# Two token tiles transposed and multiplied at a time in 64-row tiles, in an infini-attention block, with a new order of all engines

## The chip, the cores and the metric

The kernel runs on one core of a Trainium2 chip. The metric is the device time of one execution in microseconds. Five engines have their own instruction streams: TensorE (PE in the profile: matrix products and transposes, with its weight loads as PEld), VectorE (DVE), ScalarE (ACT), GpSimd (POOL) and SyncE (SP, which only issues DMA transfers here). They wait for each other through semaphores. SBUF is the on-chip memory, PSUM the eight banks that TensorE writes its results to.

## The reference

One block on a sequence of 2048 tokens of width 512: layer norm with a scale and a shift from a condition vector c, an attention of 32 heads of 16 in four segments of 512 tokens with a compressive memory, a residual; then a second such norm, a feed-forward layer of width 1792 with a squared ReLU, and a residual.

```python
x = A_x                                             # [1, 2048, 512]
mod = (_silu(c) @ w_mod).reshape(c.shape[0], 6, 1, -1)
sa, ca, ga, sb, cb, gb = (mod[:, i] for i in range(6))
h = _layernorm(x) * (1 + ca) + sa
x = x + ga * _A_ref(h, A_wq, A_wk, A_wv, A_wo, A_beta)
h = _layernorm(x) * (1 + cb) + sb
x = x + gb * _B_ref(h, B_w1, B_b1, B_w2, B_b2)

# _A_ref: q, k, v = x @ wq, x @ wk, x @ wv, cut into heads of 16 and N = 4 segments
for s in range(N):
    p = _softmax(qs @ ks.T * scale + mask)          # causal within the segment
    a_mem = (phi(qs) @ M) / (phi(qs) @ z + 1e-6)    # phi(t) = t + 1 if t > 0 else exp(t)
    o = g * a_mem + (1 - g) * (p @ vs)              # g = sigmoid(beta)
    M, z = M + phi(ks).T @ vs, z + phi(ks).sum(0)
# o of all heads, [2048, 512], times wo

# _B_ref: relu(x @ w1 + b1) ** 2 @ w2 + b2
```

## The kernel before

**Numbers.** Products are made of float32 values split into a high half, a copy rounded to a format that TensorE takes (`fp32r`), and a low half, the value less the high one. A product is three: high by high, high by low, low by high. The high copy is made by ACT, the low by DVE or POOL, so every operand of a product has a pair "hi, lo" behind it (L618 for the normed tokens, L699 for weights, L1251 and L1253 for the heads' output).

**Shapes on TensorE.** A product or a transpose works in one of three modes. F uses all 128 rows. R uses tiles of 64 rows, two side by side, which take two products at a time. C (the products of probabilities and values, L1122) uses tiles of 32 columns. The rows `128*128`, `64*128` and `128*32` of the profile show them. A transpose is a product with an identity matrix; in F a token tile (128 tokens by 512) takes four of 128x128, in R a tile of 64 rows makes one of 64x64.

**Stages.** The sequence is 16 token tiles of 128, four to a segment s = 0 to 3.
- Head: x is loaded, the modulation made (`mod_parts`, `mod_cols`: `modc` holds scale and shift by column, L586), the first segment normed and transposed (`ln1(0)`, then `ln_transposed`), the weights wq, wk, wv split (`split_w`, its lows at L699 on POOL and DVE), and the first q and k made: in F for the first unit (L779 to L781, after the last `HT`), in R afterwards (L787).
- Attention: 16 units u, four heads-groups to a segment: `qk`, `vproj`, the maxima of the scores (`a_quad`), the exponentials and the products with the values (`b_quad`), the memory (`mem`). Each unit ends in transposes of its results (L1157, `bfin`) and DVE's norm and add (L1171 to L1180). The next segment's `ln1` runs in between.
- Output product: `wo_tile` (L1226) for each token tile. Its four F transposes into a bank `bwot` (L1245), the high copy on ACT (L1251), the low on DVE (L1253), twelve F products with wo into a bank `bwop` (L1218 to L1220), the residual x1 and its statistics on DVE (L1260, L592, L593). Tiles of segments 0 to 2 load their heads' output from DRAM; those of segment 3 take it from the tile `X1L`.
- Second norm: `ln2` (L1268), four F transposes a tile (L605) and the affines half on ACT (L1281), half on DVE (L1283), into `h2raw`.
- FFN: products in a scheme like Strassen's with seven instead of eight (`ffn1`, L1475; `ffn2`, L1539 to L1541), a residual on DVE (L1550), and the stores of the output by SP (L1552). The output of segments 0 to 2 stands in tiles `X`, that of segment 3 in `X1L`.

**What sets the order.** All work is held as nodes in one `Plan` (L239): an engine, an estimated duration, the nodes it comes after, the buffers that it takes and gives back, and for TensorE the mode. A table `ORDER` (L56) lists the node numbers of PE, ACT, DVE, POOL and SP in the sequence in which that engine runs them. Buffers come from pools that are counted: `#A` 8, `#B` 8, `#V` 2 and `#D` 5 bank uses within the 8 banks, `xr` 4 token tiles, `oT` 2 split tiles of the heads' output. The transposes and products of `ln_transposed` (other than the first segment), `wo_tile` and `ln2` take banks of `#D`. A fence (L760) is a one-element copy on ACT that TensorE waits for when it goes from writing one set of row tiles to another in the same banks.

## Time and profile before

| what | us |
|---|---|
| median of three runs | 796.09 |
| lowest, highest | 795.66, 796.46 |
| profiled execution, its own time | 795.43 |
| its span (first to last instruction) | 793.7 |
| PE busy | 764.5 |
| DVE busy | 599.3 |
| ACT busy | 441.7 |
| POOL busy | 323.4 |

The busy shares of 40 equal slices of the span show the stages; the columns are tenths, PEclk the granted clock of TensorE in tenths. The FFN is the part from slice 25 on.

```profile
PE   9899999989999999999999999999999999999995
PEld 8777666765677656787576669898989889889984
DVE  5688758978789678989988789787866876476543
ACT  2568967789878898686865653556121321121110
POOL 4576674688777887545342252442002010000000
PEclk9999989999999999999999999999999999999998
DMA  9576856542644533435452275665543454544613
```

The costliest groups of instructions, busy time and mean ns, then the idle time before them with what ended it:

```profile
L899 DVE CUSTOM_DVE_ANT_0 ba<-ba,msk 128x512 f32<-128x512 f32 (+2 forms) x384 | 192.3, 533 | 36.9 <-PE ba L894 23.3
L1080 ACT ACTIVATE pt<-bpb 128x512 f32<-128x512 f32 x320 | 173.7, 619 | 22.4 <-PE bpb L1063 19.1
...
L1475 PE MATMUL bh<-H2o,w 128*128 128x256 f32 x1176 | 157.8, 282 | 1.4 <-DVE h2raw L1283 0.8
```

A row reads: line, engine, operation, tile written and tiles read (tile names without buffer numbers; `b...` is a PSUM bank), shape and type, how often it ran.

### The profile page before, as it was taken

Reading aid. Unit: us, or ns where it says so; the run is one execution under the profiler, and the core shown is the slowest. Engines: PE = TensorE matmul, PEld = TensorE weight load, DVE = VectorE, ACT = ScalarE, POOL = GpSimd, SP = SyncE. Lnnn points to the kernel's source line nnn. Section 1 sums busy time; section 2 is a strip of 40 time slices with the busy share of each in tenths; the row PEclk is TensorE's granted clock in tenths of the full one; section 3 lists DMA queues with packets and bytes.
Section 4 is the critical chain, followed back from the end, with each engine's and each line's share of the span. In section 5 each row is a group of like instructions: output and inputs, shape, how many; then the busy total and the mean of one; then the engine's idle time right before and its main releaser. Section 6 shows DMA issues by size and latency. Waiting matters only on the chain.

```text
span 793.7 us, 18015 instructions
## 1 busy us (share of the span) xinstructions
PE 764.5 (96%) x6649; PEld 606.7 (76%) x6649; DVE 599.3 (76%) x1591; ACT 441.7 (56%) x1001; POOL 323.4 (41%) x400
## 2 busy tenths in 40 slices
PE   9899999989999999999999999999999999999995
PEld 8777666765677656787576669898989889889984
DVE  5688758978789678989988789787866876476543
ACT  2568967789878898686865653556121321121110
POOL 4576674688777887545342252442002010000000
PEclk9999989999999999999999999999999999999998
DMA  9576856542644533435452275665543454544613
GB/s 313 138 195 171 246 181 196 160 135 94 192 128 133 169 94 96 131 86 159 130 141 81 82 252 199 213 239 199 186 169 116 180 204 181 186 165 160 233 53 145
DMA packets 59265, 129.65 MB, mean 163 GB/s; under 512 B 8613, under 2 KB 23977, under 8 KB 55594
## 3 DMA queue, kind: packets, MB, share of 16 engines
q1 hardware_dynamic: 59026, 128.37, 50.3%
q8 instruction: 53, 0.87, 0.5%
q14 instruction: 34, 0.28, 0.1%
q10 hardware_dynamic: 152, 0.13, 0.1%
HBM read 81.29 MB, written 20.19 MB: 128 GB/s over the span
## 4 chain that ended last, share of the span: by engine, by line
PE 61%; ACT 8%; DVE 4%; DMA 2%; SPq 1%; issue 1%; POOL 1%; ACTq 0%; DVEq 0%; POOLq 0%
PE bh L1475 16%; PE bpf L1540 6%; PE bpf L1539 6%; PE bpf L1541 6%; PE bpv L1122 5%; PE bqk L787 4%; PE bpb L1063 3%; PE ba L894 3%; ACT pt L1080 3%; PE bv L860 2%; PE bwop L1218 2%; PE bwop L1220 2%; PE bwop L1219 2%; ACT lnf L611 1%; SPq L839 1%
## 5 line engine op out<-in xcount | busy, mean ns | idle before, releaser
L899 DVE CUSTOM_DVE_ANT_0 ba<-ba,msk 128x512 f32<-128x512 f32 (+2 forms) x384 | 192.3, 533 | 36.9 <-PE ba L894 23.3
L1080 ACT ACTIVATE pt<-bpb 128x512 f32<-128x512 f32 x320 | 173.7, 619 | 22.4 <-PE bpb L1063 19.1
L1475 PEld LDWEIGHTS bh<-H2o,w 128*128 128x128 f32 x1176 | 153.9, 189 | 11.6 <-ACT h2raw L1281 1.4
L1475 PE MATMUL bh<-H2o,w 128*128 128x256 f32 x1176 | 157.8, 282 | 1.4 <-DVE h2raw L1283 0.8
L1067 POOL TENSOR_SCALAR_AFFINE_SELECT pt<-pt 128x512 f32<-128x512 f32 x128 | 79.6, 638 | 87.7 <-ACT pt L1080 65.0
L787 PE MATMUL bqk<-HT,WQK 64*128 64x512 f32 x720 | 104.4, 399 | 0.0
L1521 ACT CAST rr<-xx 128x512 fp32r<-128x512 f32 x56 | 34.4, 620 | 97.3 <-DVE xx L1511 60.2
L894 PE MATMUL ba<-ST 63*128 63x256 f32 (+2 forms) x512 | 79.7, 351 | 5.5 <-DMA ST<-sg 1.4
L1122 PE MATMUL bpv<-pt,VT 128*32 128x512 f32 (+3 forms) x1024 | 83.7, 448 | 0.7 <-POOL pt L1067 0.4
L1063 PE MATMUL bpb<-ST 64*128 64x256 f32 (+2 forms) x512 | 80.4, 352 | 2.2 <-ACT e L828 0.7
L787 PEld LDWEIGHTS bqk<-HT,WQK 64*128 64x128 f32 x720 | 73.3, 187 | 6.5
L894 PEld LDWEIGHTS ba<-ST 63*128 63x128 f32 x512 | 51.4, 186 | 31.2 <-ACT pt L1080 7.1
L1063 PEld LDWEIGHTS bpb<-ST 64*128 64x128 f32 x512 | 52.5, 188 | 21.1 <-ACT pt L1080 4.7
L1539 PE MATMUL bpf<-w,rr 128*128 128x512 f32 x160 | 63.5, 397 | 0.0
L1540 PE MATMUL bpf<-w,rr 128*128 128x512 f32 x160 | 63.0, 393 | 0.0
L1541 PE MATMUL bpf<-w,rr 128*128 128x512 f32 x160 | 62.5, 391 | 0.0
L860 PE MATMUL bv<-WVO,HT 64*128 64x512 f32 x384 | 54.9, 397 | 0.0
L899 DVE DVE_READ_ACCUMULATOR2_ANT mx<- 128x1 f32 x384 | 54.3, 141 | 0.0
L1122 PEld LDWEIGHTS bpv<-pt,VT 128*32 128x32 f32 x1024 | 27.3, 110 | 33.7 <-issue 25.5
L1523 DVE TENSOR_TENSOR rr<-xx,rr 128x512 fp32r<-128x512 f32 x56 | 40.0, 720 | 12.7 <-ACT rr L1521 12.6
L1501 ACT COPY p<-bh 128x256 f32<-128x256 f32 x28 | 10.4, 371 | 63.2 <-PE bh L1475 34.9
L1498 DVE SCALAR_TENSOR_TENSOR u<-bh,b1c,u 128x256 f32<-128x256 f32 x56 | 26.9, 480 | 24.3 <-PE bh L1475 23.2
(171 smaller groups left out, 1459.8 us busy)
## 6 DMA issues: line engine op xcount, KB each, us to landing
w<-w1d SPq DMA_DIRECT2D x28, 1792.0 KB
ST<-sg SPq DMA_DIRECT2D x192, 128.0 KB
w1d<-X1L SPq DMA_DIRECT2D x21, 512.0 KB
xt<-in_A_x SPq DMA_DIRECT2D x16, 256.0 KB
wm<-in_w_mod SPq DMA_DIRECT2D x16, 256.0 KB
xw<-in_A_x SPq DMA_DIRECT2D x16, 256.0 KB
X1L<-in_B_w SPq DMA_DIRECT2D x7, 512.0 KB
wr<-in_B_w SPq DMA_DIRECT2D x14, 256.0 KB
```

What stands on the lines that cost most here:

```text
L787: nc.tensor.matmul(bank(banks[w]), W3(w, k, x, cols.start, cols.stop)[r], HT[r, y, k], start=turn == k == i == 0, stop=turn == 1 and k == ...
L860: nc.tensor.matmul(bank(banks[t]), HT[r, x, k, (t2 + t) * P:(t2 + t + 1) * P], WVO[r, k, y], start=turn == k == i == 0, stop=turn == 1 and ...
L894: nc.tensor.matmul(dst[:, c0:c0 + n], ST[b:b + 63, 0, sl, qt * P:(qt + 1) * P], ST[b:b + 63, 1, sl, :n], start=True, stop=True)
L899: nc.vector.tensor_tensor_reduce(i, i, msk[:, 512 - n:], scale=1.0, scalar=-3e38, op0=ALU.add, op1=ALU.max, accum_out=o)
L1063: nc.tensor.matmul(dst, ST[b:b + 64, 1, sl, kb * P:(kb + 1) * P], ST[b:b + 64, 0, sl, q0:512], start=True, stop=True)
L1067: nc.gpsimd.affine_select(out=ap, in_=ap, pattern=[[0, ap.shape[1]], [1, P]], compare_op=ALU.is_ge, fill=0.0, base=0, channel_multiplier=-1)
L1080: ns = [op("ACT", 0.49, lambda j=j: nc.scalar.activation(buf("PPP"[n], pt)[:, i + j], bank(keys[j]), AF.Exp, scale=0.25), pr[slot] + 0.01 ...
L1122: nc.tensor.matmul(bank(o)[32 * hq:32 * hq + 32, q0:q0 + src.shape[1]], v[:, a:a + 32], src, start=start, stop=stop, tile_position=(0, 32 ...
L1475: nc.tensor.matmul(pb(i), A[:, x, kk], B[:, y, kk], start=kk == j == 0, stop=kk == 1 and j == 2)
L1539: nc.tensor.matmul(q, rh, wh, start=(i == 0), stop=False)
L1540: nc.tensor.matmul(q, rh, wl, start=False, stop=False)
L1541: nc.tensor.matmul(q, rl, wh, start=False, stop=(i == NF - 1))
```

## The change

Three groups of token tiles are now handled two at a time, in R.

1. `ln_pair` takes the place of two `ln_transposed` for segments 1 to 3. The transposes of two tiles are one turn of 16, of 64 rows by 128, into two banks: the upper 64 rows of both tiles go to one, the lower to the other. ACT makes the affine of a whole bank, copies the high half into HT in strides, and POOL makes the low half.
2. `wo_pair` takes the place of two `wo_tile` for segments 0 to 2: two loads of heads, two of x; 16 R transposes into two banks; high and low copies per bank; 48 R products of 64 rows by 512 in two turns, with a fence between the turns. In the first turn the rows of tile half j go to bank j, in the second to the other. The pool `oT` has one tile, of twice the size. Tiles of segment 3 keep `wo_tile`.
3. `first_pair` transposes the second norm of segment 0 in two pairs.

In `ln_transposed` the low half is locked in the plan (`lock=True`), and the table `ORDER` is new for all engines.

In instructions: transposes of the first norm of 128x128 (bank `blnq`, from `xt`) 64 to 16, of 64 rows 0 to 96; of the second norm 64 to 48 and 0 to 32; of the output product (bank `bwot`, from `ot`) 48 to 0 and 0 to 96; products with wo of 128 rows 192 to 48, of 64 rows 0 to 288; one-element copies of the fence on ACT 8 to 14. All other counts stay. Along PE's order the shape changes 181 times before and 136 times now.

```diff
 ORDER = {
     "PE": """
-8-27 3 28-40 86 94 111 41 88 42-45 96 46-51 123 52 105 53 117 54-77 280-281 290 282-284 291-292 285 293 286 294 287
+8-20 3 21-38 105 111 94 86 39 96 88 40-52 117 53-56 123 57-70 290 71-73 291-292 74-77 293 280-282 294 283-287 295-297
...
-             "phi1": 2, "pk": 1, "am": 3, "on": 1, "mx": 2, "mt": 1, "oT": 2, "mv": 2, "ac": 1, "#F": 4, "xx": 3, "rr": 4, "wr": 3,
+             "phi1": 2, "pk": 1, "am": 3, "on": 1, "mx": 2, "mt": 1, "oT": 1, "mv": 2, "ac": 1, "#F": 4, "xx": 3, "rr": 4, "wr": 3,
...
-        l = op(low, 1.24 if low == "POOL" else 0.6, lambda: ln_split(dst(), t, TL[f], low)[1](), pr + 0.03, after=[h], put=[f])
+        l = op(low, 1.24 if low == "POOL" else 0.6, lambda: ln_split(dst(), t, TL[f], low)[1](), pr + 0.03, after=[h], put=[f], lock=True)
...
+    def ln_pair(s, g, src, sc, bi, pr, after, put, wait):
+        b, f = ([(n, sc, s, g, j) for j in (0, 1)] for n in ("lnq", "lnf"))
+        def turn():
+            for k in range(KD):
+                for i in (0, 1):
+                    for j in (0, 1):
+                        r, c_ = slice(64 * j, 64 * j + 64), k * P + 64 * i
+                        nc.tensor.transpose(bank(b[j])[:, c_:c_ + 64], src(i)[r, k * P:(k + 1) * P], ident[r, r])
+        n = pe("R", 0.522, turn, pr, after=after, get=[("#D", q) for q in b], put=put)
+        ends = []
+        for j in (0, 1):
+            a = op("ACT", 1.38, lambda j=j: ln_affine("av", buf("oraw", f[j]), bank(b[j]), sc, bi), pr + 0.01 + 0.01 * j,
+                   after=[n, *MODC[sc], *(wait if j else [])], get=[("oraw", f[j])], put=[b[j]])
...
+            h = act(512, lambda part=part, whole=whole: nc.scalar.copy(part(0), whole()), pr + 0.02 + 0.01 * j, sbuf=True,
+                    after=[a, *wait], put=[f[j]])
+            l = op("POOL", 1.24, lambda part=part, whole=whole: nc.gpsimd.tensor_tensor(part(1), whole(), part(0).bitcast(F32), op=ALU.subtract),
+                   pr + 0.03 + 0.01 * j, after=[h], put=[f[j]])
+            ends += [h, l]
+        return ends, a
...
+    def wo_pair(g, pr):
...
+        n = pe("R", 0.522, turn, pr, after=ld, get=[("#D", q) for q in b], put=o)
...
+        for j in (0, 1):
+            h = act(512, lambda j=j: nc.scalar.copy(part(0, j), whole(j)), pr + 0.01 + 0.005 * j, after=[n] + hl[:1],
+                    get=() if j else [("oT", ot)], put=[b[j]])
+            hl += [h, dve(512, lambda j=j: nc.vector.tensor_tensor(part(1, j), whole(j), part(0, j).bitcast(F32), op=ALU.subtract),
+                          pr + 0.012 + 0.005 * j, after=[h], put=[b[j]])]
+        def mm(turn, k):
+            for i, (x, y) in enumerate(((0, 0), (0, 1), (1, 0))):
+                for j in (1, 0) if turn else (0, 1):
+                    t, r = j ^ turn, slice(64 * j, 64 * j + 64)
+                    nc.tensor.matmul(bank(bo[t]), TL[ot][r, x, k, t * P:(t + 1) * P], WVO[r, k, y],
+                                     start=turn == k == i == 0, stop=turn == 1 and k == 0 and i == 2)
+        n = None
+        for turn_ in (0, 1):
+            for k in range(KD):
+                if turn_ and not k:
+                    n = fence(WVO[64:65, KD - 1, 0, :1], pr + 0.04, n)
+                n = pe("R", 0.697, lambda turn_=turn_, k=k: mm(turn_, KD - 1 - k if turn_ else k), pr + 0.03 + 0.02 * turn_ + 0.002 * k,
+                       after=[n] if n else [*hl, *WON], get=() if turn_ or k else [("#D", q) for q in bo],
+                       put=[ot] if turn_ and k == KD - 1 else ())
...
     for s in range(NS - 1):
         for t in range(4):
-            wo_tile(4 * s + t, e + K_P[s] + 0.3 * t)
+            if t % 2:
+                wo_pair(4 * s + t - 1, e + K_P[s] + 0.3 * t)
```

Where the order differs, at the three places that the prediction speaks of. First DVE in the head, around the modulation columns (`modc`), the normed tiles (`xt`), the affines out of the transposes' banks (`lnf`) and the low halves (`HT`). Before:

```order
L586 TENSOR_SCALAR modc<-bmodc 128x4
L601 TENSOR_SCALAR xt<-xt,mv 128x512
L586 TENSOR_SCALAR modc<-bmodc 128x4
L601 TENSOR_SCALAR xt<-xt,mv 128x512
L613 TENSOR_SCALAR lnf<-blnq,modc 128x128 x2
L601 TENSOR_SCALAR xt<-xt,mv 128x512
L613 TENSOR_SCALAR lnf<-blnq,modc 128x128 x6
L618 TENSOR_TENSOR HT<-lnf,HT 128x4x128 x4
L699 TENSOR_TENSOR WVO<-w,WVO 128x4x128
```

Now:

```order
L586 TENSOR_SCALAR modc<-bmodc 128x4 x2
L613 TENSOR_SCALAR lnf<-blnq,modc 128x128 x4
L601 TENSOR_SCALAR xt<-xt,mv 128x512 x2
L618 TENSOR_TENSOR HT<-lnf,HT 128x4x128
L613 TENSOR_SCALAR lnf<-blnq,modc 128x128 x4
L618 TENSOR_TENSOR HT<-lnf,HT 128x4x128 x3
L733 TENSOR_TENSOR WVO<-w,WVO 128x4x128
```

Both columns stand ahead of the affines, one low half stands between the two halves of the affines, and three follow them.

Second PE at the seam between the attention and the FFN: the last products with values (`bpv`), the transposes of the last heads (`bfin`), those of the second norm (`blnq` from `xh`), and the output product of segment 3 (`bwot` from `X1L`, then `bwop`). Before:

```order
L1122 MATMUL bpv<-pt,VT_114 32x256 x4
L605 MATMUL blnq<-ident,xh 128x128 x4
L1218 MATMUL bwop<-WVO,oT 128x512
L1219 MATMUL bwop<-WVO,oT 128x512
L1220 MATMUL bwop<-WVO,oT 128x512
L1157 MATMUL bfin<-ident,oraw 128x64 x16
L1218 MATMUL bwop<-WVO,oT 128x512
L1219 MATMUL bwop<-WVO,oT 128x512
L1220 MATMUL bwop<-WVO,oT 128x512
```

Nine of these last products stand behind the heads' transposes, and then the transposes of `X1L`. Now:

```order
L1191 MATMUL bfin<-ident,oraw 128x64 x16
L1156 MATMUL bpv<-pt,VT_114 32x512 x4
L1156 MATMUL bpv<-pt,VT_114 32x384 x4
L1156 MATMUL bpv<-pt,VT_114 32x128 x4
L1156 MATMUL bpv<-pt,VT_114 32x256 x4
L1366 MATMUL blnq<-ident,xh 128x64 x16
L1191 MATMUL bfin<-ident,oraw 128x64 x16
L1279 MATMUL bwot<-ident,X1L 128x128 x16
L1252 MATMUL bwop<-WVO,oT 128x512
```

The products of the earlier tiles stand further ahead; behind the last heads' transposes come those of `X1L`.

Third SP at the end: the last loads of weights (`w`) and the stores of the output, of segments 0, 1 and 2 (`X_6369`, `X_6370`, `X_6371`) and of segment 3 (`X1L`). Before:

```order
L1425 DMA w_10592<-w1d_136 128x3584
L1552 DMA out<-X_6369 128x512
L1425 DMA w_10700<-w1d_137 128x3584
L1552 DMA out<-X1L 128x256
L1552 DMA out<-X_6369 128x512
L1552 DMA out<-X_6371 128x512 x2
L1552 DMA out<-X1L 128x512 x3
L1552 DMA out<-X_6370 128x512 x3
L1552 DMA out<-X_6371 128x512
```

Now, with the segments in `X_6413`, `X_6414` and `X_6415`:

```order
L1545 DMA w_10863<-w1d_136 128x3584
L1672 DMA out<-X_6413 128x512
L1545 DMA w_10974<-w1d_137 128x3584
L1672 DMA out<-X_6415 128x512
L1672 DMA out<-X_6414 128x512
L1672 DMA out<-X_6415 128x512
L1672 DMA out<-X1L 128x512
L1672 DMA out<-X1L 128x256
L1672 DMA out<-X_6415 128x512
L1672 DMA out<-X1L 128x512 x2
```

Three stores of earlier segments stand ahead of the first of `X1L`, and eight stores instead of eleven follow the last weight load.

More of the change, by code (lines that the diff above doesn't have):

```diff
@@ L225 @@
+2833 2843 2838 2842 2851-2852 2847 2856 2860 2865 2861 2869 2874 2870 2905 2879 2878 2883 3171-3174 3129 3175-3177
+3428-3431 3132 3432-3434 3685-3687 3383 3386 3643 3688-3689 3389 3135 3690 3126 3691 3649 3392 3646 3900 3906 3640
+3903 3897
 """,
@@ L669, in ln1 @@
                    after=[r[t // n]], put=[mv, ("xt", g)], lock=True)
-            HTN[s] += ln_transposed(s, t, lambda g=g: TL["xt", g], lambda: HT, ("phi0", "phi1", "phi1", "oraw")[t] if s == 0 else "oraw", CA, SA, p_turn[t], [a],
-                                    [("xt", g)], HUSE[s - 1], "POOL" if s else "DVE", "#D" if s else "#A")
+            ap = (ap if t % 2 else []) + [a]
+            if s and t % 2:
+                e_, gate_ = ln_pair(s, t - 1, lambda i, g=g: TL["xt", g - 1 + i], CA, SA, p_turn[t], ap + ([gate_] if t > 1 else []), [("xt", g - 1), ("xt", g)],
+                                    HUSE[s - 1])
+                HTN[s] += e_
+            elif not s:
+                HTN[s] += ln_transposed(s, t, lambda g=g: TL["xt", g], lambda: HT, ("phi0", "phi1", "phi1", "oraw")[t] if s == 0 else "oraw", CA, SA, p_turn[t], [a],
+                                    [("xt", g)], HUSE[s - 1], "DVE", "#A")
     ln1(0, PR0 + 0.3, [PR0 + 0.4 + 0.004 * (t % 2) + 0.05 * (t // 2) for t in range(4)])
```

362 lines of the change are left out of this document (208 added, 154 removed), and 8 rows, old and new, of the table ORDER.

## The prediction

> **What bounds the kernel now.** I read the shares of busy time first, and then the busy time of each engine in stretches cut at the stages. The columns of the second view are PE, PE's weight loads, DVE, ACT and POOL (busy us and instructions), the granted TensorE clock, the share of DMA and GB/s.
>
> ```profile
> PE 764.5 (96%) x6649; PEld 606.7 (76%) x6649; DVE 599.3 (76%) x1591; ACT 441.7 (56%) x1001; POOL 323.4 (41%) x400
> ```
> ```profile
> 0.00:36.50 36.50, 31.20 (x237) 29.15 (x237) 21.01 (x37) 13.87 (x28) 18.89 (x36) 0.95 0.81 246
> 36.50:140.00 103.50, 99.86 (x1054) 73.88 (x1055) 80.21 (x248) 77.63 (x194) 67.05 (x75) 0.97 0.63 190
> ...
> 340.00:440.00 100.00, 99.07 (x932) 69.53 (x928) 89.56 (x276) 71.22 (x158) 39.52 (x56) 1.00 0.44 123
> ...
> 479.00:784.70 305.70, 304.24 (x1912) 272.97 (x1910) 210.79 (x413) 85.70 (x170) 36.87 (x30) 1.00 0.48 172
> ```
>
> TensorE is the bound: 764.5 of 793.7 us. In the FFN it is idle 1.46 of 305.70 us at full clock, and that stage's products don't change, so nothing is won or lost there but a shift of its start. In the attention it is nearly as full, with DVE next (89.56 of 100). Three places are left: the head, where PE is busy on warming products and then waits; the turns between tile shapes in the attention; and the tail behind PE's last product. I price the change there.
>
> **The head.** Its rows:
>
> ```profile
> 25.45 0.38 PE L779 MATMUL bqk<-HT,WQK 128*128 128x256 f32 x1
> 29.23 0.38 PE L780 MATMUL bqk<-HT,WQK 128*128 128x256 f32 x1 [3.40 <-DVE HT L618]
> ...
> 36.54 3.01 PE L787 MATMUL bqk<-HT,WQK 64*128 64x512 f32 x24
> 39.40 1.57 PE L860 MATMUL bv<-WVO,HT 64*128 64x512 f32 x12
> ```
> ```profile
> 17.05 0.16 DVE L586 TENSOR_SCALAR modc<-bmodc 128x4 f32<-128x4 f32 x1 [1.17 <-PE bmodc L584]
> ...
> 23.86 5.31 DVE L618 TENSOR_TENSOR HT<-lnf,HT 128x512 fp32r<-128x512 f32 x4 [1.96 <-ACT HT L618]
> 29.10 1.78 DVE L699 TENSOR_TENSOR WVO<-w,WVO 128x512 fp32r<-128x512 f32 x1
> ```
> ```profile
> L618 DVE TENSOR_TENSOR HT<-lnf,HT 128x512 fp32r<-128x512 f32 x4 | 5.3, 1386 | 2.0 <-ACT HT L618 2.0
> ...
> L1253 DVE TENSOR_TENSOR oT<-bwot,oT 128x512 fp32r<-128x512 f32 x16 | 10.8, 683 | 1.8 <-ACT oT L1251 1.8
> ```
> ```profile
> 31.98 2.56 POOL L699 TENSOR_TENSOR WVO<-w,WVO 128x512 fp32r<-128x512 f32 x2
> ```
> ```profile
> 38.49 7.85 SPq L839 DMA_DIRECT2D ST<-sg  x12
> ```
> ```profile
> 29.80:33.20 3.40, 3.40 (x18) 3.40 (x17) 2.63 (x5) 0.00 (x0) 3.40 (x3) 0.50 0.28 66
> 23.40:29.20 5.80, 2.43 (x21) 2.17 (x19) 5.34 (x5) 5.80 (x12) 5.12 (x4) 1.00 0.98 201
> ```
>
> PE waits 3.40 us for DVE's low halves of HT (L618): four of 1386 ns each in a row, 23.86 to 29.17. All four come after the last affine, and POOL is busy with weights' lows for 5.12 of the same 5.80 us. The same 128x512 subtraction from PSUM (L1253) takes 683 ns.
>
> The Trainium skill, "SBUF — State Buffer", section "Who interferes with whom", says that a DVE instruction with two SBUF inputs contends with a GpSimd one that reads SBUF, and one with at most one such input doesn't; the 1386 against 683 ns agrees. By that rule alone each low that still overlaps POOL stays at 1386, and two that don't would gain 1.4 us.
>
> The new order puts tile 0's low right behind its own affines instead of behind the last ones, has the two modulation columns (L586) ahead of every affine, and loads wq's first block ahead of token tiles 2 and 3. The columns come about 1 us sooner (one L601 less ahead, one PE turn less between them), and the run of four lows loses one; the 1.96 us in which DVE waited at 23.86 for ACT fills with it. 1.0 + 1.39 + 1.96 = 4.4, or 5.5 if one more low escapes POOL's part (0.7) and the affines close up (0.4): that much earlier the last low ends. Behind the wait PE ran at half clock, 29.80 to 33.20, where full clock does the same in 1.7 less; with a shorter wait that goes too. So the top is 5.5 + 1.7, and 1.3 more if the first products run while the later lows are made, 8.5; the bottom is 3.0, nearly the 3.40 alone, if what comes next is as late as before. What comes next: WVO's lows, on POOL until 34.5, and the twelve fills of ST (38.49, 7.85 us of SP) that feed the first scores. I take 7.2 less 0.7 for these: **−6.5**.
>
> **The turns of the attention.** Rows of PE around a token tile of the output product; the second number is the row's time, and I use starts:
>
> ```profile
> 392.23 0.39 PE L1220 MATMUL bwop<-WVO,oT 128*128 128x512 f32 x1
> 392.45 0.60 PE L1245 MATMUL bwot<-ident,ot 128*128 128x128 f32 x4
> 392.81 0.48 PE L1218 MATMUL bwop<-WVO,oT 128*128 128x512 f32 x1
> ...
> 394.05 0.40 PE L1220 MATMUL bwop<-WVO,oT 128*128 128x512 f32 x1
> 394.38 1.03 PE L1063 MATMUL bpb<-ST 64*128 64x512 f32 x8
> 395.34 0.50 PE L1218 MATMUL bwop<-WVO,oT 128*128 128x512 f32 x1
> 395.68 0.40 PE L1219 MATMUL bwop<-WVO,oT 128*128 128x512 f32 x1
> 395.91 0.40 PE L1220 MATMUL bwop<-WVO,oT 128*128 128x512 f32 x1
> ...
> 396.94 0.71 PE L1157 MATMUL bfin<-ident,oraw 64*128 64x64 f32 x16
> 397.46 0.77 PE L1063 MATMUL bpb<-ST 64*128 64x256 f32 x8
> ```
>
> Two products of one shape start 0.23 apart (395.68, 395.91). From full tiles to row tiles it is 0.33 (394.05 to 394.38), and the first after the way back takes 0.34 (395.34 to 395.68). So a turn into and one out of row tiles cost 0.10 and 0.11 here; some of it lies at the other shape's start too, which these rows don't part. I take 0.2 a turn, between 0.1 (what is seen at one side) and 0.25. Along PE's order the shape changes 181 times before and 136 times after: 45 × 0.2 = **−9.0** (−4.5 to −11.3).
>
> Transposes: a token tile takes 0.36 (392.45 to 392.81), two take 0.72; sixteen of 64 rows, as the new pairs, take 0.52 (396.94 to 397.46). 14 pairs × −0.20 = **−2.8**. Products of a pair: 24 × 0.233 = 5.59 in full tiles, and 24 row products in 2.86 (36.54 to 39.40), so 48 in 5.72: 6 × 0.13 = **+0.8**. The six new one-element copies on ACT (the fence between the two turns) make PE wait for ACT's queue, each with scores or transposes put between in PE's order. I cost them at 0, since a product in flight is 0.2 to 0.4 and the cover 0.5 to 1.0. Gone, they cost 0.6 each, 3.6 in all. The copy waits on ACT for the first turn's last product, and behind it stand the exponentials that the next PV products need.
>
> **The seam into the FFN.** Before, nine products of 0.23 stand between the last head's transposes and the ones that need the finished heads; the DVE's work behind:
>
> ```profile
> 467.50 0.49 PE L1245 MATMUL bwot<-ident,X1L 128*128 128x128 f32 x3
> 469.31 1.64 PE L1245 MATMUL bwot<-ident,X1L 128*128 128x128 f32 x13 [1.32 <-DVE X1L L1180]
> ```
> ```profile
> 465.29 0.72 DVE L1283 TENSOR_SCALAR h2raw<-blnq,modc 128x128 f32<-128x128 f32 x2
> 465.92 0.26 DVE L1171 RECIPROCAL bfin<-bfin 128x16 f32<-128x16 f32 x1
> ...
> 467.72 1.53 DVE L1180 TENSOR_TENSOR X1L<-X1L,am 128x512 f32<-128x512 f32 x1
> ```
>
> After, those products are gone from there (they come earlier), and sixteen transposes of 1.0 us with the bank's four affines (2 × 0.72) are ahead of the chain reciprocal, products, add: 1.44 + 1.8 + 1.53 = 4.8 us in which PE has about nothing, against 1.3 and a little now: **+3.5** (+1 if the affines come while PE still has products, +5.2 with a half-clock stretch like that of the head, 1.7, behind it). Mid and seam together −9.0 − 2.8 + 0.8 + 3.5 = **−7.5**, ±4 for waits that a new order can make or end, half-clock stretches among them:
>
> ```profile
> 104.90:111.70 6.80, 6.41 (x66) 4.69 (x65) 3.70 (x14) 5.16 (x12) 3.36 (x4) 0.50 0.43 144
> ...
> 285.80:289.20 3.40, 3.24 (x28) 1.63 (x28) 2.36 (x10) 2.63 (x7) 2.12 (x4) 0.50 0.16 40
> ```
>
> These two cost up to half of 10.2 us, 5.1, and nothing in the rows says that an order keeps them.
>
> **The tail.**
>
> ```profile
> 784.30 0.39 PE L1541 MATMUL bpf<-w,rr 128*128 128x512 f32 x1
> ```
> ```profile
> 783.47 0.33 SPq L1552 DMA_DIRECT2D out<-X1L  x1
> ```
> ```profile
> 785.50:789.80 4.30, 0.00 (x0) 0.00 (x0) 0.00 (x0) 0.00 (x0) 0.00 (x0) 0.74 1.02 380
> 789.80:791.70 1.90, 0.00 (x0) 0.00 (x0) 0.00 (x0) 0.00 (x0) 0.00 (x0) 0.50 1.02 381
> 791.70:793.70 2.00, 0.00 (x0) 0.00 (x0) 0.00 (x0) 0.00 (x0) 0.00 (x0) 0.50 0.01 3
> ```
>
> PE ends at 784.7; the DMA engines then work full at 380 GB/s until 791.7. SP's order explains it: behind the last weight load stands a store of X1L that waits for its sum until 783.47, and ten more stores stand behind it, 10.5 × 262 kB in all = 2.75 MB, 7.2 us. After, three stores of earlier segments stand ahead of the first of X1L, which comes sooner, and about five stores (1.31 MB, 3.4 us from 783.5 at the earliest) are left: the bytes end at 787 to 787.5, and with the same 2.0 us the span at 789.5: **−4.2** (−3.3 to −5.1).
>
> **Sum.** −6.5 − 7.5 − 4.2 = −18.2. The profiled execution took 795.43 us (span 793.7), so 777.2; the median of the runs, 796.09, stands 0.7 above it: **778 us**.
>
> **Rivals.** A pair that stalls (slower): a pair takes two banks at once for its transposes and two for its products, of a pool of five, and there is one oT tile where there were two, so the next pair, the LN transposes and the heads' own banks wait for its copies. Each has two DVE lows of 683 ns behind two ACT copies; if PE stands still for them, 1.4 us × 14 pairs = 19.6, and the time is 797. It decides from 1.3 us a pair on. Against it: the order has scores and head products between the transposes and the products, and DVE has 10 of 100 us free. The Trainium skill, "TensorEngine Tiling (Array Packing)", Gotcha 1: PSUM Pressure, says that different row tiles write to different banks and can't be in one bank at the same time. That asks for the two banks of a pair; the sixteen row transposes of 396.94 show no wait inside, and no run here shows what the pools then lack. Only part lands: DVE, not PE, sets the attention's pace in places (89.56 of 100), and then the turns' 9.0 are worth a third (−3.0 − 2.8 + 0.8 + 3.5 = −1.5), and the fills of ST hold the first scores, so that the head gives 3.0: −3.0 − 1.5 − 4.2 = −8.7, 787, and up to 793 with the stalls of the ±4 on top. More lands: the two half-clock stretches go too, 5.1, the seam costs 1 instead of 3.5, and the head gives 8.5 instead of 6.5: 778 − 9.6 = 768 and below. That the change doesn't do what it says, since a pair's transposes wait for the later of its two tiles and the shapes alternate as before: then the 9.0 are 0, which is the second case too.
>
> **The numbers.** Forecast as summed, with its own errors 768 to 787: 0.70. Part of it, 787 to 794: 0.13. More, 760 to 768: 0.08. The stall, 795 or more: 0.09, of which 0.02 within the 0.2% (1.6 us) that a measurement here can tell from no change. So faster by over 0.2% 0.91, within 0.02, slower 0.07. The range that leaves out no more than 2 in 10: 768 to 789, the low end from the bounds of turns and waits (−2.0 head, −2.3 turns, −4 waits, −0.9 tail), the high end into the second case.
>
> **What would show it.** Head: the first row product of L787's counterpart starting near 30 instead of 36.54, no wait of 3.40 on HT, and no half clock behind. Turns: in the attention, PE's busy time falling by about 11 us; if instead idle time grows with releasers among the copies of oT or the fence, the stall is right. Seam: an idle of PE of 4 us or more behind the heads' last transposes. FFN: again about 305 us. Tail: 5 us from PE's last product to the end instead of 9. I would be wrong if the head is held by loads (its DMA share is 0.81 already), or if the fences cost PE over 0.6 each.

## The result, and the profile after

The changed kernel takes 784.45 us (median of 4 runs, 781.83 to 786.04) against 796.22 for the kernel before (4 runs, 795.66 to 796.46): a ratio of 0.985, 95% interval 0.9819 to 0.9881. The forecast was 778, with a range of 768 to 789. Three later groups of runs give 783.97, 785.98 and 783.83, with 796.88, 796.92 and 796.69 before. So the change gains 11 to 13 us; the sum said 18.2.

The profiled execution took 786.04 us, the slowest of its four. Its busy times, and its busy times by stage, in the columns of the prediction's second view:

```profile
PE 760.5 (97%) x6905; PEld 613.1 (78%) x6905; DVE 590.1 (75%) x1591; ACT 445.4 (57%) x1007; POOL 325.0 (41%) x400
```
```profile
0.00:31.05 31.05, 29.15 (x238) 27.28 (x238) 14.39 (x33) 13.98 (x28) 15.66 (x35) 1.00 0.87 288
31.05:134.55 103.50, 101.08 (x1100) 74.85 (x1101) 81.66 (x258) 80.77 (x200) 70.63 (x77) 0.98 0.65 189
340.00:440.00 100.00, 99.35 (x1100) 75.90 (x1100) 92.01 (x279) 75.89 (x171) 40.20 (x57) 1.00 0.48 136
474.50:780.10 305.60, 305.28 (x1918) 274.01 (x1916) 211.23 (x415) 86.56 (x171) 39.63 (x31) 1.00 0.50 180
780.10:784.30 4.20, 0.00 (x0) 0.00 (x0) 0.66 (x1) 0.00 (x0) 0.00 (x0) 0.92 0.33 125
```

In the attention PE's busy time was to fall by about 11 us; over the whole span it fell by 4.0 (764.5 to 760.5). The head ends 5.5 us earlier, the FFN keeps its 305.6, and the tail is 4.2 instead of 9. What fails is the part between. Here is the whole middle, from the first row product of q and k to the first product of the FFN, before:

```profile
36.50:478.90 442.40, 428.93 (x4502) 304.44 (x4502) 366.71 (x1142) 342.16 (x803) 267.53 (x335) 0.98 0.50 148
```

and after:

```profile
31.05:474.50 443.45, 426.09 (x4752) 311.84 (x4752) 363.79 (x1146) 344.89 (x808) 269.69 (x336) 0.97 0.51 147
```

It is no shorter: 442.40 and 443.45. The granted clock (third column from the right) has dropped from 0.98 to 0.97, and the windows show where. These are, in the changed kernel, the stretches at half clock in the middle, each with the 3.4 us ahead of it:

```profile
66.80:70.20 3.40, 2.97 (x47) 1.84 (x46) 3.27 (x15) 3.34 (x9) 2.73 (x4) 1.00 0.91 277
70.20:73.60 3.40, 3.40 (x29) 1.71 (x28) 2.79 (x12) 3.40 (x9) 3.19 (x4) 0.50 0.79 225
165.80:169.20 3.40, 1.67 (x11) 0.83 (x10) 3.21 (x6) 2.43 (x7) 2.66 (x3) 1.00 0.73 187
169.20:176.00 6.80, 5.04 (x49) 2.99 (x52) 4.86 (x18) 6.01 (x16) 5.79 (x7) 0.50 0.30 101
206.70:210.10 3.40, 1.22 (x14) 0.71 (x10) 2.79 (x6) 1.69 (x6) 0.88 (x2) 1.00 0.42 153
210.10:213.50 3.40, 3.40 (x31) 1.55 (x30) 0.90 (x3) 1.91 (x5) 2.84 (x4) 0.51 0.01 2
275.00:278.40 3.40, 2.92 (x27) 1.75 (x25) 1.41 (x4) 3.37 (x8) 2.17 (x5) 1.00 0.91 280
278.40:288.60 10.20, 10.05 (x63) 4.76 (x64) 5.64 (x23) 8.58 (x20) 5.32 (x7) 0.50 0.33 84
292.10:295.50 3.40, 2.61 (x31) 1.83 (x28) 3.19 (x10) 3.19 (x10) 3.15 (x7) 1.00 0.00 0
295.50:298.90 3.40, 3.40 (x23) 1.51 (x25) 1.72 (x5) 2.42 (x6) 2.88 (x5) 0.50 0.25 50
462.70:466.10 3.40, 0.94 (x9) 0.94 (x10) 2.27 (x6) 1.59 (x5) 2.80 (x2) 1.00 0.94 343
466.10:469.50 3.40, 3.40 (x13) 2.91 (x12) 2.25 (x4) 3.40 (x8) 1.38 (x2) 0.51 0.93 305
```

That is 30.7 us at half clock in the middle (stretch × 2 × (1 − mean granted clock)) against 13.7 before. Ahead of three of the six PE stood still for half of the 3.4 us or more; ahead of the other three it was busy for 2.6 to 2.97.

**Head.** The low halves of HT on DVE, then POOL's work beside them, then the first row product on PE:

```profile
18.53 0.69 DVE L618 TENSOR_TENSOR HT<-lnf,HT 128x512 fp32r<-128x512 f32 x1
...
21.56 0.69 DVE L618 TENSOR_TENSOR HT<-lnf,HT 128x512 fp32r<-128x512 f32 x1
...
23.41 1.29 DVE L618 TENSOR_TENSOR HT<-lnf,HT 128x512 fp32r<-128x512 f32 x2 [1.16 <-ACT HT L618]
```
```profile
19.71 1.27 POOL L733 TENSOR_TENSOR WQK<-w,WQK 128x512 fp32r<-128x512 f32 x1 [3.19 <-ACT WQK L729]
25.74 1.29 POOL L733 TENSOR_TENSOR WQK<-X1L,WQK 128x512 fp32r<-128x512 f32 x1 [4.76 <-DMA xt<-in_A_x]
```
```profile
31.05 3.01 PE L821 MATMUL bqk<-HT,WQK 64*128 64x512 f32 x24
```

The lows of one trace after the other, first before, then now (shortest, median and longest in ns):

```profile
L618 DVE TENSOR_TENSOR HT<-lnf,HT x4: 680/1553/1757, 23.9 to 27.4; 128x512 fp32r<-128x512 f32 x4
L618 DVE TENSOR_TENSOR HT<-lnf,HT x4: 685/689/693, 18.5 to 24.0; 128x512 fp32r<-128x512 f32 x4
```

All four now take 0.69 us, 2.76 us together instead of 5.31, each at a time when POOL is idle (3.19 us before 19.71, 4.76 before 25.74). The Trainium skill, "SBUF — State Buffer", section "Who interferes with whom", says that a DVE instruction with two SBUF inputs contends with a GpSimd one that reads SBUF. The trace agrees: before, three of the four began with POOL at work, now none does. The prediction let two of them gain.

**Seam.** PE, then DVE, at the heads' end:

```profile
460.53 0.69 PE L1191 MATMUL bfin<-ident,oraw 64*128 64x64 f32 x16
461.15 0.55 PE L1279 MATMUL bwot<-ident,X1L 128*128 128x128 f32 x3
465.16 2.12 PE L1279 MATMUL bwot<-ident,X1L 128*128 128x128 f32 x13 [3.46 <-DVE X1L L1214]
```
```profile
460.95 1.38 DVE L1375 TENSOR_SCALAR h2raw<-blnq,modc 128x128 f32<-128x128 f32 x4
...
464.05 1.06 DVE L1214 TENSOR_TENSOR X1L<-X1L,am 128x512 f32<-128x512 f32 x1
```

PE waits 3.46 us instead of 1.32, behind the bank's four affines and the chain after them, and half clock follows.

**Tail.** SP's stores of the output; PE ends at 780.03:

```profile
748.31 1.68 SPq L1672 DMA_DIRECT2D out<-X  x3
775.21 2.51 SPq L1672 DMA_DIRECT2D out<-X1L  x2
777.76 0.45 SPq L1672 DMA_DIRECT2D out<-X  x1
779.40 1.72 SPq L1672 DMA_DIRECT2D out<-X1L  x2
```

Two stores of `X1L` wait for PE's last sums; nothing else is left behind them.

### The profile page after: what moved, and what is told of

Read it like the earlier page. It is cut to its first block, busy times and chain, and to the rows that moved or that the text cites. A ratio compares the mean times of both kernels' runs of the same rounds, so it can differ in the third digit from the quotient of the medians.

```text
span 784.3 us, 18545 instructions
## 1 busy us (share of the span) xinstructions
PE 760.5 (97%) x6905; PEld 613.1 (78%) x6905; DVE 590.1 (75%) x1591; ACT 445.4 (57%) x1007; POOL 325.0 (41%) x400
## 4 chain that ended last, share of the span: by engine, by line
PE 59%; DVE 2%; ACT 2%; DMA 1%; issue 1%; POOL 1%; SPq 0%; ACTq 0%; DVEq 0%; POOLq 0%
PE bh L1595 17%; PE bpf L1660 6%; PE bpf L1659 6%; PE bpf L1661 6%; PE bpv L1156 4%; PE bwop L1337 4%; PE bqk L821 3%; PE bpb L1097 3%; PE ba L928 2%; PE bv L894 1%; DMA w<-w1d 1%; PE blnq L605 1%; ACT pt L1114 1%; PE bwop L1252 1%; PE bwop L1253 1%
## 5 line engine op out<-in xcount | busy, mean ns | idle before, releaser
L933 DVE CUSTOM_DVE_ANT_0 ba<-ba,msk 128x512 f32<-128x512 f32 (+2 forms) x384 | 192.1, 533 | 44.6 <-PE ba L928 24.7
L1114 ACT ACTIVATE pt<-bpb 128x512 f32<-128x512 f32 x320 | 172.1, 609 | 18.2 <-PE bpb L1097 17.2
L1595 PEld LDWEIGHTS bh<-H2o,w 128*128 128x128 f32 x1176 | 155.5, 189 | 11.0 <-DVE xx L1618 0.6
L1595 PE MATMUL bh<-H2o,w 128*128 128x256 f32 x1176 | 159.5, 282 | 0.2 <-DMA w<-w1d 0.2
L1156 PE MATMUL bpv<-pt,VT 128*32 128x256 f32 (+3 forms) x1024 | 87.9, 462 | 0.5 <-DVE den L1028 0.4
L1097 PE MATMUL bpb<-ST 64*128 64x384 f32 (+2 forms) x512 | 83.1, 356 | 5.0 <-ACT mt L995 2.2
L928 PE MATMUL ba<-ST 63*128 63x256 f32 (+2 forms) x512 | 83.4, 354 | 3.6 <-ACT pt L1114 1.0
L928 PEld LDWEIGHTS ba<-ST 63*128 63x128 f32 x512 | 54.8, 192 | 25.6 <-ACT pt L1114 6.2
L1433 POOL TENSOR_TENSOR tt<-h2raw 128x512 f32<-128x512 f32 x8 | 12.3, 1547 | 112.0 <-ACT h2raw L1400 52.1
L1156 PEld LDWEIGHTS bpv<-pt,VT 128*32 128x32 f32 x1024 | 28.0, 112 | 35.0 <-issue 24.2
L1643 DVE TENSOR_TENSOR rr<-xx,rr 128x512 fp32r<-128x512 f32 x56 | 40.5, 727 | 10.6 <-ACT rr L1641 10.6
```

Of the source, the lines that this page charges most:

```text
L928: nc.tensor.matmul(dst[:, c0:c0 + n], ST[b:b + 63, 0, sl, qt * P:(qt + 1) * P], ST[b:b + 63, 1, sl, :n], start=True, stop=True)
L933: nc.vector.tensor_tensor_reduce(i, i, msk[:, 512 - n:], scale=1.0, scalar=-3e38, op0=ALU.add, op1=ALU.max, accum_out=o)
L1097: nc.tensor.matmul(dst, ST[b:b + 64, 1, sl, kb * P:(kb + 1) * P], ST[b:b + 64, 0, sl, q0:512], start=True, stop=True)
L1114: ns = [op("ACT", 0.49, lambda j=j: nc.scalar.activation(buf("PPP"[n], pt)[:, i + j], bank(keys[j]), AF.Exp, scale=0.25), pr[slot] + 0.01 ...
L1156: nc.tensor.matmul(bank(o)[32 * hq:32 * hq + 32, q0:q0 + src.shape[1]], v[:, a:a + 32], src, start=start, stop=stop, tile_position=(0, 32 ...
L1595: nc.tensor.matmul(pb(i), A[:, x, kk], B[:, y, kk], start=kk == j == 0, stop=kk == 1 and j == 2)
```

## The experiments

Times are medians, with the number of runs. The single tiles, the tail alone and the head alone ran on one chip, beside the kernel before (796.88) and the changed one; the idle time filled and the two repairs on a second (796.92); the two other fills and head with tail on a third (796.69). Two tables gather all traces first, since each experiment is read against them. The first gives the stages in us, cut at PE's first row product (end of the head), at the first product of the FFN and at the end of the last product:

```
order in the middle  kernel                head    middle (at half clock)  FFN     tail
before               before                36.54   442.37 (13.7)           305.78  9.01
before               tail alone            37.08   441.20 (13.7)           306.26  4.33
before               head alone            30.93   440.43  (6.8)           306.15  8.97
before               head and tail         31.99   442.41 (17.1)           306.21  4.26
changed              changed               31.05   443.48 (30.7)           305.50  4.30
changed              changed again         31.71   441.38 (30.7)           305.00  4.30
changed              changed, third        30.97   440.23 (23.9)           304.83  4.30
changed              changed, fourth       31.82   441.46 (27.3)           304.95  4.29
changed, singles     single tiles          31.08   457.05 (23.9)           304.77  4.29
changed              idle time filled      30.82   440.54 (13.7)           306.45  4.29
changed              fill sized            32.00   439.54 (20.5)           306.10  4.30
changed              more fill             32.14   443.82 (20.5)           306.03  4.29
changed, maxima      maxima first          31.61   437.54 (23.9)           305.27  4.30
changed, repaired    repaired              30.80   441.81 (30.7)           305.89  4.30
```

And the middle up to the first transposes of `X1L` taken apart: each start-to-start time on PE is set against the median, at full clock, of the same pair of shapes. The sum of all medians and of all excess at full clock is the first number, the excess in half-clock stretches the second. The last column counts PE's changes of shape there:

```
                    full clock   excess at half   turns
before              421.4         9.6             178
tail alone          421.3         8.5             178
head alone          424.8         4.2             178
head and tail       419.8        11.2             178
changed             410.7        19.5             133
changed again       407.9        20.1             133
changed, third      411.8        15.0             133
changed, fourth     410.5        17.5             133
single tiles        429.4        14.7             213
```

The split is an estimate. Where a pair that straddles the edge of a stretch is counted, and whether pairs are told apart by their banks too, moves the difference between the two kernels from 9 to 12 us in the first number and from 7 to 10 in the second; their sum is the measured time.

**Single tiles.** The order of the changed kernel, with each pair done as two single tiles by the code of before, in the pair's place. So that it can run in that order, the load of an output tile is split in two and two buffers are taken later:

```diff
-            af = [op("ACT", 1.38, lambda: ln_affine("av", buf(pool, f), bank(b), sc, bi), pr + 0.01, after=[n, *MODC[sc]], put=[b])]
+            af = [op("ACT", 1.38, lambda: ln_affine("av", buf(pool, f), bank(b), sc, bi), pr + 0.01, after=[n, *MODC[sc]], get=[(pool, f)], put=[b])]
...
-        ld = sp(load, pr - 0.2, 1 << (18 if last else 19), 1 if last else 2, after=heads + [N_FFN if last else N_LATE],
-                get=[("xr", xk)] if last else [("xr", o), ("xr", xk)])
+        ld = sp(load_x1 if last else load, pr - 0.2, 1 << 18, after=heads + [N_FFN if last else N_LATE],
+                get=[("xr", xk if last else o)])
```

> The order of the changed kernel, with every pair taken apart again into two single tiles in full tiles (64 more transposes of 128x128 for 224 fewer of 64 rows, 144 more products of 128 rows for 288 fewer of 64, 45 or so more turns of shape, no fence). Theory A, the pairs save the 10 us of TensorE work in the attention that was forecast and it is given back in stretches at half clock that the new order brings: about 10 us slower than the changed kernel, 793 to 797, with as many stretches at half clock (25 to 31 us). Theory B, turns of shape cost next to nothing since DVE sets the pace: within 3 us of the changed kernel. Theory C, the half-rows of the pairs themselves bring the half clock: stretches at half clock fall to 17 us or less and the time is 785 to 789.

Measured: 799.14 us (12), a ratio of 1.004 to before (1.0015 to 1.0066), 15.2 above the changed kernel on that chip. The middle:

```profile
31.10:488.10 457.00, 441.46 (x4496) 310.04 (x4496) 363.79 (x1146) 344.56 (x802) 269.61 (x336) 0.97 0.50 143
```

So the pairs pay, more than the 10 us that the expectation named (it counted 45 turns; there are 80), and this order with single tiles in the pairs' places is slower than the kernel before. At full clock the middle costs 429.4 against 410.2 (mean of the changed kernel's four) for 80 more turns; without the 2.0 that transposes and products differ by, 17.2 / 80 = 0.21 us a turn, if nothing but turns differs there. Against the order of before (421.8, mean of four) it is 7.6 for 35 turns, 0.22. Half clock comes where the changed kernel has it (70.3, 172.7, 213.6, 281.9, 479.9 against 70.2, 169.2, 210.1, 278.4, 466.1): so for the most part the order brings it, not the 64-row tiles. Over all runs on that chip the mean time at half clock is 24.2 us with single tiles and 30.5 with pairs.

**The tail alone, the head alone, both.** The first is the kernel before with the four stores of `X1L` moved behind the seven of earlier segments in SP's order; the second has the new order for all that starts before 34 us; the third has both.

```diff
-3902 3122 3645 3642 3899 3893 3896 3388 3382 3385 3639
+3122 3645 3642 3388 3382 3385 3639 3902 3896 3893 3899
```
```diff
-8-27 3 28-40 86 94 111 41 88 42-45 96 46-51 123 52 105 53 117 54-77 280-281 290 282-284 291-292 285 293 286 294 287
+8-20 3 21-38 105 111 94 86 39 96 88 40-52 117 53-56 123 57-70 290 71-73 291-292 74-77 293 280-282 294 283-287 295-297
...
```

> The kernel before with one thing changed: in SyncE's order the last four stores of segment 3 stand behind the seven of the earlier segments. Theory A, the tail was stores queued behind one that waits for its sum: the stretch from PE's last product to the end falls from 9.0 to 4 to 5 us, 791 to 792. Rival, the bytes only move to where the last weights are loaded and delay TensorE: 795 or more.

> The kernel before with the changed kernel's order for the work of the head alone (all that it starts before 34 us), the rest in the old order. Theory A, what the head gains reaches the end: the first row product at 31 instead of 36.5 and 789 to 791.5. Rival, the fills of ST and the weights' low halves are as late as before and the rest waits: 794 or more.

> The kernel before with the head's order of e3 and the stores' order of e2 together: single tiles and the old order for everything between. Theory A, the pairs' 10 us are given back at half clock, so that head and tail alone (-5.5 and -4.6 in the traces, and less half clock in the head) make as much as the whole change: 783 to 787, within 2 us of the changed kernel. Rival, pairs and the new order of the middle still carry some 3 to 5 us of the gain: 788 to 790.

Measured: the tail alone 790.72 (10), ratio 0.9923 (0.9897 to 0.9949); the head alone 789.15 (7), 0.9921 (0.9889 to 0.9952); both 786.09 (6), 0.9863 (0.9839 to 0.9887). In the traces the tail falls from 9.01 to 4.33 and the head from 36.54 to 30.93, as in the changed kernel:

```profile
784.50:786.50 2.00, 0.04 (x1) 0.00 (x0) 0.77 (x2) 0.00 (x0) 0.00 (x0) 1.00 0.96 353
786.50:788.90 2.40, 0.00 (x0) 0.00 (x0) 0.00 (x0) 0.00 (x0) 0.00 (x0) 0.96 0.15 58
```
```profile
30.93 1.43 PE L786 MATMUL bqk<-HT,WQK 64*128 64x512 f32 x10
```

The first fence is the tail alone (PE ends at 784.55, and the execution ends 4.3 us behind it instead of 9.0), the second the head alone. The medians' gains, 6.2 and 7.7, don't add to the 10.6 of both; in the traces the middle of the head alone had only 6.8 us at half clock, that of both 17.1. The run that matters is the third: head and tail are 10.6 of the gain, and beside it the whole change, with all its pairs, took 783.83 (5). The rest of the change is worth 2.3 us, about the 2 that were expected at most.

**The changed kernel again**, three times, as the measure for the others:

> The changed kernel as it is, for its spread. Theory A, its time follows how long TensorE ran at half clock, half a microsecond lost for each: 781 to 787, and the runs ordered by their mean granted clock, 0.002 of it worth about 1.5 us. Rival, the spread comes from transfers: no order by the clock.

> The changed kernel as it is, on the chip of the three others, to compare them with: 783 to 786.

> The changed kernel as it is, on the chip of the three others, to compare them with: 782 to 787.

Measured 783.97 (4), 785.98 (6), 783.83 (5). The runs do follow the clock, at a lower price than the 0.5 that was expected: over the 19 runs of the changed kernel, each group against its own mean, a us more at half clock goes with 0.35 us more time (correlation 0.90). The middle is 441.6 us in the mean of the four traces, and 441.6 in the four traces with the order of before.

**Idle time filled.** Identity products into a bank that the next step of PE overwrites, at the seam (24) and ahead of the step that waits 1.30 us at 167 us (10):

```diff
+    def warm(n, count):
+        f, key = n.fn, n.get[0][1]
+
+        def go():
+            for _ in range(count):
+                nc.tensor.matmul(bank(key)[:, :P], ident, ident, start=True, stop=True)
+            f()
+        n.fn = go
+    warm(PL.nodes[2795], 24)
+    warm(PL.nodes[1132], 10)
```

> The changed kernel with 34 products of the identity with itself put in (128x128, 0.12 us each), whose results are overwritten: 24 ahead of the transposes of X1L at the seam, where TensorE waits 3.5 us for DVE, and 10 ahead of the transposes of phi of unit 5, where it waits 1.3 us for a bank. No useful work is added or moved, so the waits stay. Theory A, half the clock is the price of idle stretches, and TensorE kept busy keeps it: no stretch at half clock behind the seam and one or two fewer between 165 and 181 us, 2 to 5 us faster than the changed kernel on the same chip. Rival, the waits alone cost the time and the half clock is a side sight: the same or up to 2 us slower.

Measured: 785.30 (6), 0.7 below the changed kernel's 785.98 on that chip, within the spread of both (783.85 to 787.39, 782.07 to 787.82), where 2 to 5 were expected. PE at the seam:

```profile
457.86 5.62 PE L1696 MATMUL bwot<-ident 128*128 128x128 f32 x48
463.33 1.91 PE L1279 MATMUL bwot<-ident,X1L 128*128 128x128 f32 x16
```

The stretches at half clock behind the filled places are gone (466 and 169 us), and over all runs the mean time at half clock falls from 32.4 to 20.9 us. The seam decides it: all four traces of the changed kernel have a stretch at half clock behind it, and none of the four in which products were put there (24, 12, 12 and 18) has. So PE without work does bring half clock there. But the 24 products are 48 rows of 0.117 us and overrun the wait that they fill by 5.62 − 3.46 = 2.16, and the ten others take 2.50. In the trace the middle is 1.1 shorter than the mean of the changed kernel with 14.5 us less at half clock: 1.1 + 2.16 + 2.50 = 5.8, or 0.40 us for one at half clock, if none of the 2.50 was hidden. The wait there, 1.0 to 1.4 us in the four traces, is gone from the list of waits; if the ten products hid all of it, the price is 0.30.

**Fill sized, and more of it.** 12 and 5 products in place of 24 and 10; then ten more at four further places:

```diff
-    warm(PL.nodes[2795], 24)
-    warm(PL.nodes[1132], 10)
+    warm(PL.nodes[2795], 12)
+    warm(PL.nodes[1132], 5)
```
```diff
+    warm(PL.nodes[502], 2)
+    warm(PL.nodes[1239], 3)
+    warm(PL.nodes[2080], 3)
+    warm(PL.nodes[1726], 2)
```

> As e5, with half the products, since each was two rows of 0.12 us there and the 48 at the seam took 5.6 us where 3.5 were idle: 12 ahead of the transposes of X1L (24 rows, 2.8 us) and 5 ahead of those of phi of unit 5 (10 rows, 1.2 us). Theory A: the clock stays full behind both as in e5, and the filling now costs nothing: 2 to 4 us faster than the changed kernel on the same chip, its time at half clock 8 to 12 us less. Rival, what e5 left at half clock was made up by nothing but chance: within 1 us.

> As e9, with ten more such products ahead of four other steps of the attention, where stretches with little array work are followed by half the clock in most traces: 2 ahead of scores of unit 1 (68 us), 3 ahead of the transposed maxima of unit 6 (207 us), 3 ahead of a pair of the first norm (275 us), 2 ahead of the transposed maxima of unit 9 (293 us). Theory A: 20 rows, 2.4 us at most, against some 14 us at half clock: 3 to 6 us faster than the changed kernel on the same chip. Rival, here TensorE isn't idle long enough and the rows cost what they take: no faster than e9, or 1 to 2 us slower than it.

Measured: 785.96 (6) and 787.56 (6), beside 783.83 for the changed kernel; mean time at half clock 24.0 and 21.5 against 27.2, where the first was to save 8 to 12 us of it and 2 to 4 us of time. At the seam of the first the products now fit:

```profile
459.72 2.94 PE L1696 MATMUL bwot<-ident 128*128 128x128 f32 x24
462.51 0.49 PE L1279 MATMUL bwot<-ident,X1L 128*128 128x128 f32 x3
463.76 1.64 PE L1279 MATMUL bwot<-ident,X1L 128*128 128x128 f32 x13 [0.76 <-DVE X1L L1214]
```

Yet nothing is gained, and at 171 us the stretch at half clock stays with five products. Where the seam's wait is filled the FFN takes 305.9 to 306.5, in the changed order without filling 304.8 to 305.5: about 1 us of what the seam wins comes back there. The second kernel is 3.7 us slower than the changed one (782.53 to 790.93) and 1.6 slower than the first, no more than its ten further products take (20 rows, some 2.4 us). As a repair, filling fails.

**Waits repaired in the order.** First, the copies of a head's scores ahead of an affine on ACT, and its mask earlier on POOL, so that the maxima come sooner; then, beside that, the activation that makes `mt` ahead of a split on ACT, two affines behind `X1L`'s add on DVE, and 18 products at the seam:

```diff
-1471 1089 1088 1472 843 842 223 1474-1475 1133-1134 1333 1336 1335 727 1339 1342 226 1480 1483 991-992 1481 1341 1484
+1089 1088 1471-1472 843 842 223 1474-1475 1133-1134 1333 1336 1335 727 1339 1342 226 1480 1483 991-992 1481 1341 1484
...
-1490 240 1150 1163 1162 1165-1166 1404 1403 1495 1497 1240-1241 1170 1169 1172-1173 1160 243 1177-1178 1501 1359 1358
+1490 240 1150 1163 1162 1165-1166 1404 1403 1240-1241 1495 1497 1170 1169 1172-1173 1160 243 1177-1178 1501 1359 1358
```

> The changed kernel with one knot of its order undone: for unit 5 ACT copies the scores of the maxima before it makes the affine of a pair (two copies of 0.54 ahead of 1.5 us of affine), and POOL masks them before the two rows that it had ahead. Theory A, that knot is what makes TensorE wait 1.3 us for the bank at 166 us, and brings the half clock behind it: the wait is gone, 1 to 4 us faster than the changed kernel on the same chip. Rival, the bank is freed by something else: the wait stays and the time is within 1 us.

> The change of e6, and with it: for unit 6 ACT copies the transposed maxima before it splits q (it stood behind a split that waits for the buffer sg), DVE makes the last two affines of the second norm after the add of X1L instead of before the last heads' norm, and 18 products of the identity stand ahead of the transposes of X1L. Theory A, each takes a wait or a half-clock stretch away: the wait at the seam falls from 3.5 to 2.6 us, no half clock behind it, 4 to 8 us faster than the changed kernel on the same chip, 776 to 780. Rival, waits only move to the next engine: within 2 us of it.

Measured: 785.30 (6; 780.43 to 789.45) and 783.59 (6; 782.66 to 787.12), beside 785.98; expected were gains of 1 to 4 and of 4 to 8 us. The waits that were aimed at are shorter or gone in the list of PE's waits of the repaired kernel, whose columns are total, times and longest (three lines of it):

```profile
PE ba L928 <- ACT lnf L611: 1.0, 1, 1.0
PE bpkt L1046 <- DVE mx L933: 0.8, 1, 0.8
PE bh L1595 <- DVE H2o L1449: 0.8, 1, 0.8
```

The seam's 3.46 is not in it, and a wait of the FFN's first products is. The wait for the bank at 167 us is 0.8 in both traces, but the half clock behind it is no shorter (10.2 us in both; 6.8 or 10.2 in the changed kernel's four). In the trace of the repaired kernel the middle took 441.81 with 30.7 us at half clock. Of its six runs this has the most of it: their mean time at half clock is 25.3, against 32.4 for the changed kernel, which goes with the 2.4 us of the medians but is within the spread of the times. No version that was tried beats the changed kernel by more than the spread.

## Why the prediction was right, and which step was wrong

The time lies in the range, on the side and in the case that was called likeliest, but the sum is 6.4 us too large. It was right by its ends: head, tail and FFN give −11.1, while the turns with the seam, forecast at −7.5 ± 4, came to 0.0 (a middle of 441.6 us before and after), outside their own bounds. That the total stayed in the range without this term is in part luck. By its terms, with the mean of the changed kernel's four traces against the two with the head of before, or the four with its middle:

```
term                        forecast   measured
head                        -6.5       -5.4   (36.8 to 31.4)
turns, transposes, products -11.0      -11.6  (421.8 to 410.2 at full clock)
seam                        +3.5       +2.0   (11.4 to 13.4, from X1L's first transposes to the FFN)
half clock, up to the seam   0         +9.6   (8.4 to 18.0)
FFN                          0         -1.0   (306.1 to 305.1)
tail                        -4.2       -4.7   (9.0 to 4.3)
sum                         -18.2      -11.1
```

**The head** was right in its place and near in size. The columns, the affines and the lows moved as said, the wait of 3.40 on HT is gone, and so is the half clock behind it. The step on the lows had one of them leave the run and perhaps another escape POOL; all four did. It read 1386 ns as the time of each low; that is the mean of 0.68 to 1.76 us, and the one of 0.68, at 26.82, began while POOL stood still (26.35 to 27.03).

**The turns** were right. The price of 0.2 was chosen between 0.1 and 0.25; taking the pairs apart gives 0.21 and 0.22. The sign that was named for them, 11 us less busy time of PE in the attention, did not come (428.93 to 426.09 in the middle); the 17 us more at half clock hide up to half of their length of it. The rival in which DVE sets the pace and the turns are worth a third falls: at full clock 9 to 12 us arrive, and without the pairs the same order is 15.2 us slower. The stalling pair falls too: in the list of PE's waits, which starts at 0.15 us, none ends on a copy of oT, and the two that end on a fence's copy come to 0.5 us.

**The seam** was right in kind: 4.8 us of nearly idle PE was forecast, 3.46 came, with half clock behind it. The FFN takes back 1.0, which was not foreseen; that it goes with the seam's wait is seen in the traces with and without filling, but its cause was not looked into.

**The wrong step** is the last one of the mid term: "±4 for waits that a new order can make or end, half-clock stretches among them", with zero as its middle. I had seen two stretches there and counted them only as 5.1 us that might go. In place of that the time at half clock up to the seam rose from 12.8 to 24.7 us (means of four), and the excess in these stretches by 9.6. Half of 11.9 is 6.0, the most that the clock alone can cost; the other 3.6 would be waits that stand inside these stretches. The turns saved 11.6, and this with the seam's 2.0 took all of it back, which is why head and tail alone reach 786.09 and the whole change 783.83.

How much of the 9.6 would come back if the clock stayed full is not settled. Across 48 runs of the kernel before, each of three groups against its own mean, a us more at half clock goes with 0.34 us more time (correlation 0.80), the changed kernel's runs give 0.35, and the filled run 0.30 to 0.40; for 15.4 us in the whole middle (28.2 against 12.8) that is 5 to 6 us of the 7.5 that the middle fell short. No run here kept the changed order and the full clock at no cost, so this stays an estimate.

## What to carry to other kernels

Price a turn of PE between tile shapes (a change from tiles of one shape to another) from the start-to-start times in the trace; here 0.2 us held against both the old and the new order. When an order packs PE's work more tightly in one place, look for the places that it empties: here a stretch of 3.4 us with little work on the array cost its idle time and then up to half of the next 3.4. And test a change of several parts by giving the old kernel the cheap parts alone: here the ends, which touch a few rows of the order, are four fifths of the gain.

## What the runs showed of the hardware

Stretches at half clock that end within the span are multiples of 3.41 us, and in each trace they lie on one grid from the first to the last. The Trainium skill, "TensorE: Matmul & The Clock Gate", Part 1, has a free-running window of 3413 ns and half rate after an idle one. The grid agrees; a wholly idle window is not needed. In 66.80:70.20 PE is busy 2.97 of 3.40 us and half clock follows. Each product can be weighted by the share of the array that it uses (its columns at the 0.233 us that 512 of them take in these traces, times the tile's rows and columns over 128 x 128). From 25 us on, the fourteen traces then sort by the work that starts in a window at full clock: under 0.25 of it, the next window was at half clock in 27 of 27 cases; from 0.25 to 0.35 in 29 of 86; from 0.35 to 0.39 in 1 of 37; above that in 2 of about 2840. That is a rule read off these traces, tested only by the filled runs. Small tiles count for little in it: the stretch at 66.80, with 0.31 by this count, holds scores and products of 64 and 32 rows or columns.

An identity product of 128x128 in float32 shows as two rows of 0.117 us, so a filler takes twice the time that its count suggests. And a 128x512 subtraction of two SBUF tiles on DVE took 0.69 us when it ran or began with POOL idle, and 1.35 to 1.76 us when POOL was already at work.
